# Products of zeros ahead of TensorE's first work, and behind the stages of the first two tiles

## The chip, the cores and the metric

The kernel runs on one core of one Trainium2 chip. The metric is device time in microseconds (us); lower is better. Names of engines in the profile: PE is TensorE (PEld its weight loads), DVE is VectorE, ACT is ScalarE, POOL is GpSimd, SP is the engine that issues most transfers.

## The reference, cut to what matters

Three layers follow one another: an attention-like recurrence over 768 steps (4 batches, 8 heads, head size 48), a feed-forward layer with an ELU, and a layer of 8 experts of which every token takes the best one.

```python
for t in range(S):
    kt, vt, rt, wt = (k[:, :, t], v[:, :, t], r[:, :, t], w[:, :, t])
    cur = np.einsum('bhd,bhe->bhde', u[None] * kt, vt)
    y[:, :, t] = np.einsum('bhd,bhde->bhe', rt, state + cur)
    state = wt[:, :, :, None] * state + np.einsum('bhd,bhe->bhde', kt, vt)
...
h = x @ w_in
g = np.where(h > 0.0, h, alpha * (np.exp(np.minimum(h, 0.0)) - 1.0))
return (g @ w_out).astype(np.float32)
...
h = np.maximum(x[mask] @ w1[e], 0.0)
out[mask] = gate_w[mask, None] * (h @ w2[e])
```

The weights of the feed-forward layer come as 64-bit floats and are turned into pairs of 16-bit floats on the chip.

## The kernel before

**Tiles and steps.** The recurrence is cut into 24 tiles of 128 steps by one batch (6 chunks by 4 batches). A tile goes through four steps. A1 (kind 0) forms running products of the decay by a scan (L336 on DVE, `RK`) and their inverses (L341, L342). A2 (kind 1) scales keys and queries on POOL (L386), forms the diagonal term by products of two columns (L395) and transposes the keys (L401). A3 (kind 2, the scores) multiplies keys and queries (L424) and masks the result on DVE (L433, into `Ab` or a spare place that the program calls `ohp` or `gg`). A4 (kind 3, the output) multiplies the masked scores with the values (L461), adds the state's part (L474, from the second chunk on), gathers the result on DVE (L478, `y`), turns it into the feed-forward layer's input (L485 on ACT, L487 on POOL, L363 on PE, L364 on ACT) and renews the state (L497). The products of the first eight tiles are of 32-bit floats.

**The feed-forward layer** works on groups of two tiles. A group takes eight units; a unit is 18 products of 256 columns (L514, `psf<-xT,wi`), an ELU on ACT and DVE (L520 to L524) and 12 products of 384 columns (L536, `pso<-wo,ring`). During the first group the weights are converted too, 16 pieces. A piece costs DVE two times three instructions (L275, L276, L277, from `stg` by `pso` into `sti`), and then ACT two (L289, L292) and POOL one (L293). A unit can't begin before its pieces are done.

**Order.** The code lists tile 0 and tile 1 step by step (`ORD`, with `P` for a piece of weights) and then the units of the first group, among them the steps of the tiles that follow. The framework's scheduler then sets each engine's own order by a modelled time line, and every engine runs its list strictly in that order. A row that waits holds up all that stand behind it on its engine.

**PSUM.** `psum(tag)` hands out banks by tag: two of `f`, three of `a`, one each of `o0`, `o1`, `o2`. The pieces use `o2`; the first group's outputs use `o0` and `o1`.

**Spare room.** `spare(n)` cuts columns from places that are idle in the first stage; the place that the program calls `X` (`X_101`) is one of them.

Of the kernel before, what the change touches and what calls it, by code (L numbers as in the profile page):

```python
# [49 lines left out]
def _pow2(n):  # L50
    return float(2.0 ** n)
# [77 lines left out]
def body(ctx, tc, r, k, v, w, u, w_in, w_out, mod, w_gate, bias, w1, w2, cst, out, dbg=None):  # L129
    nc = tc.nc  # L130
# [8 lines left out]
    def cc(name):  # L139
        o, n = _CW[name]  # L140
        return cs[:, o:o + n]
# [4 lines left out]
    def psum(tag):  # L146
        if tag == "o":
            tag = f"o{on_[0] % 3}"
            on_[0] += 1
        return ps.tile([128, 512], F32, tag=tag, name="ps" + tag, bufs=BK[tag])  # L150
# [34 lines left out]
    def spare(n, first=0):  # L185
        for z_, a_ in list(enumerate(arenas))[first:]:
            o = anext[z_]
            if o + n <= a_.shape[1]:
                anext[z_] += n
                return a_[:, o:o + n]  # L190
        raise ValueError(n)
# [15 lines left out]
    Ss = [p1.tile([PT, 2, QH, D], F16, name=f"Ss{i}") for i in range(1)]  # L207
    Z128 = p1.tile([PT, B, QH], F32, name="Z128")

    def setup():  # L210
        nc.scalar.preload_act_table_set("natural_log_exp_and_others")
        nc.scalar.dma_start(cs, cst)
        nc.scalar.dma_start(u2, u)
        nc.vector.tensor_copy(id16, cc("ident"))
        nc.gpsimd.memset(nel, -_pow2(PH))
        nc.vector.memset(bnd, 0.0)
        nc.vector.memset(bnd[:, 0::HW], _pow2(SR))
        nc.gpsimd.memset(run_, 0.0)

    def setup2():  # L220
        nc.vector.tensor_copy(tri16, cc("tri"))
# [84 lines left out]
    def load(i, which="wkrv"):  # L306
        c, b = divmod(i, B)
        st = T.setdefault(i, {})
        for nm, src in (("w", w), ("r", r), ("k", k), ("v", v)):
            if nm not in which or nm in st:  # L310
                continue
            if nm == "v":
                t = ev_[i] if i in ev_ else l4.tile([128, H, D], F32, tag="lv", name="lv")
            elif nm == "w":
                t = ld.tile([PT, 2, QH, HW], F32, tag="lw", name="lw")
            else:
                t = l3.tile([PT, QH, C], F32, tag="l" + nm, name="l" + nm)
            nc.sync.dma_start(t, src[i])
            st[nm] = t
# [580 lines left out]
    def moe_block(j, nt=2, hook=None, done=0, ahead=0, conv=False, load=False, x=False):  # L900
# [38 lines left out]
        if x and j == NB - 2:  # L939
            moe_gather(NB)  # L940
            moe_gather(NB + 1)
            moe_xm(NB)

    setup()
    NTL = NC_ * B
    xT = {}
# [6 lines left out]
    def at_step(kind, i):  # L953
        step(kind, i)
        if kind == (LK if i >= EAR else LE) and i + 2 < NTL:
            load(i + 2)

    def step(kind, i):
        if kind == 0:
            A1(i)  # L960
        elif kind == 1:
            A2(i)
        elif kind == 2:
            A3(i)
        else:
            g = grp[i]
            t0, nt = GR[g]
            if i == t0:
                xT[g] = b2.tile([128, 2 * KD, 128 * GT], F16, tag="xT", name="xT", bufs=4)
            A4(i, xT[g], 128 * (i - t0))  # L970

    U_ = 3.96
    start, tt = [], 0.0
# [22 lines left out]
        load(i, "w")  # L996
    for i in range(2):
        load(i)
    for u_ in range(NU + LAG):
        if u_ < NU:  # L1000
            SEQ.append((0, u_))
        if u_ >= LAG:
            SEQ.append((1, u_ - LAG))
# [4 lines left out]
    def pre(key):  # L1008
        while pq[0] <= SEQ.index(key):
            z_, i = SEQ[pq[0]]  # L1010
            (prep_out if z_ else prep_in)(i)
            pq[0] += 1
# [12 lines left out]
    for o in ORD:  # L1025
        if o == "P":
            pre((0, n_))
            n_ += 1
        else:
            at_step(int(o[0]), int(o[1:]))  # L1030
    mp = mb = None
    NG = len(GR)
    LU = (NG - 1) * NU
# [150 lines left out]
```

## Time and profile before

| what | us |
|---|---|
| three runs | 798.78, 787.71, 795.93 |
| median of the three | 795.93 |
| profiled execution, its own time | 793.34 |
| its span, first to last instruction | 791.6 |
| outside the span | 1.7 |

The profile is of one execution. Its share of busy time by engine: PE 93%, DVE 66%, ACT 62%, POOL 51%. In a timeline row the first number is the start in us from the span's start, the second the time that the merged instructions took; x is how many records there are (a product of 32-bit floats leaves two records each), and in brackets stands the engine's idle time ahead of it and what ended it. In a table of windows an engine's number is its busy time in the stretch, with the count of records, and PEclk is TensorE's granted clock as a share of full speed, where a record of it exists.

### The profile page before, as it was taken

How to read it: one execution, taken by the hardware profiler on the slowest of the kernel's cores; microseconds unless marked ns; L12 is line 12 of the kernel's file. 1: busy time of each engine (PE TensorE's matmuls, PEld its weight loads, DVE VectorE, ACT ScalarE, POOL GpSimd, SP SyncE). 2: the span in 40 equal slices, each digit the busy share in tenths (PEclk: the TensorE clock that was granted, in tenths of full speed). 3: DMA queues.
4: the chain of work that ended last, by engine and by line, in shares of the span. 5: the costliest groups of instructions: out<-in, count | busy, mean ns of one | idle time of the engine just before them, and what ended most of it. 6: DMA issues, size and time to landing. Idle time of an engine off the chain costs nothing.

```text
span 791.6 us, 17925 instructions
## 1 busy us (share of the span) xinstructions
PE 734.1 (93%) x6963; PEld 562.0 (71%) x6963; DVE 521.8 (66%) x1076; ACT 491.8 (62%) x954; POOL 403.9 (51%) x392
## 2 busy tenths in 40 slices
PE   4799999999999899999999999999995799999984
PEld 4677877877777677767776777776773577777763
DVE  6989963465766755575557544687797467766751
ACT  3577764555666566656665765567756477777852
POOL 4888884566676677747776652012016334322220
PEclk9999999999999899989999999999999799999998
DMA  9875422232213233333232111169439998998720
GB/s 282 253 229 180 141 52 59 65 81 60 70 51 76 76 76 57 77 85 66 67 72 65 22 21 32 52 194 301 165 136 348 256 279 246 288 282 234 254 108 12
DMA packets 86611, 108.29 MB, mean 137 GB/s; under 512 B 60437, under 2 KB 66618, under 8 KB 86516
## 3 DMA queue, kind: packets, MB, share of 16 engines
q1 hardware_dynamic: 82208, 96.46, 43.5%
q0 software_dynamic: 3456, 10.24, 4.4%
q8 instruction: 58, 0.95, 0.5%
q10 hardware_dynamic: 852, 0.34, 0.2%
q14 instruction: 37, 0.30, 0.1%
HBM read 83.80 MB, written 9.84 MB: 118 GB/s over the span
## 4 chain that ended last, share of the span: by engine, by line
PE 49%; DMA 11%; DVE 6%; issue 3%; ACT 2%; POOL 0%; SPq 0%; POOLq 0%; ACTq 0%
PE pso L536 13%; PE psf L514 13%; PE pso L867 8%; PE psf L847 7%; DMA out_dram<-ob,idxb 5%; PE psa L847 2%; DMA wi<-in_w_dram 2%; DMA XM<-G 1%; PE psa L427 1%; PE psa L395 1%; DMA G<-scr,idxb 1%; DVE W L839 1%; PE psa L477 1%; PE psa L497 1%; DMA SG<-in_w_dram 1%
## 5 line engine op out<-in xcount | busy, mean ns | idle before, releaser
L514 PE MATMUL psf<-xT,wi 128*128 128x256 f16 x1728 | 214.6, 279 | 1.0 <-ACT xT L364 0.9
L536 PE MATMUL pso<-wo,ring 128*128 128x384 f16 x1152 | 214.0, 331 | 0.2
L514 PEld LDWEIGHTS <-wi 128*128 128x128 f16 x1728 | 169.2, 101 | 30.5 <-issue 1.8
L536 PEld LDWEIGHTS <-ring 128*128 128x128 f16 x1152 | 112.7, 100 | 64.0 <-issue 4.6
L522 DVE SCALAR_TENSOR_TENSOR e<-e,psf 128x512 f32<-128x512 f32 x96 | 65.6, 684 | 121.0 <-ACT e L521 105.2
L847 PEld LDWEIGHTS <-W 128*128 128x128 f16 x1008 | 93.7, 99 | 32.8 <-issue 14.9
L322 POOL TENSOR_TENSOR ring<-e,ring 128x512 f16<-128x512 f32 x80 | 93.3, 1167 | 44.9 <-ACT ring L524 29.4
L867 PE MATMUL pso<-W,gg 128*128 128x384 f16 x624 | 111.0, 326 | 3.4 <-DVE gg L322 2.9
L524 ACT ACTIVATE ring<-e 128x512 f16<-128x512 f32 x96 | 60.3, 628 | 55.8 <-DVE e L522 55.1
L867 PEld LDWEIGHTS <-gg 128*128 128x128 f16 x624 | 60.2, 98 | 39.3 <-DVE gg L322 4.2
L520 ACT ACTIVATE e<-psf 128x512 f32<-128x512 f32 x96 | 56.3, 587 | 38.9 <-PE psf L514 38.6
L847 PE MATMUL psf<-XM,W 128*128 128x256 f16 (+1 forms) x540 | 62.1, 267 | 14.4 <-DMA XM<-G 12.3
L521 ACT ACTIVATE e<-e,nel 128x512 f32<-128x512 f32 x96 | 69.0, 719 | 2.3
L875 POOL DMA_INDIRECT out_dram<-ob,idxb x20 | 27.8, 1392 | 82.5 <-DVE ob L874 40.3
L839 DVE SCALAR_TENSOR_TENSOR W<-SG,W 128x768 f16<-128x768 f32 x56 | 52.9, 955 | 18.3 <-ACT W L838 17.0
L322 DVE TENSOR_TENSOR gg<-mt,gg 128x256 f16<-128x256 f32 (+1 forms) x112 | 43.8, 402 | 30.8 <-ACT gg L854 29.4
L839 DVE SCALAR_TENSOR_TENSOR W<-wi,W 128x768 f16<-128x768 f32 x56 | 52.7, 954 | 12.1 <-ACT W L838 11.0
L838 ACT ACTIVATE W<-SG 128x768 f16<-128x768 f32 x56 | 46.2, 839 | 15.1 <-DMA SG<-in_w_dram 10.9
L853 ACT ACTIVATE mt<-psf 128x256 f32<-128x256 f32 (+1 forms) x84 | 30.0, 361 | 39.2 <-PE psf L847 24.1
L838 ACT ACTIVATE W<-wi 128x768 f16<-128x768 f32 x56 | 46.0, 840 | 11.6 <-DMA wi<-in_w_dram 5.2
L371 POOL TENSOR_TENSOR rkp<-lr,lk 112x512 f32<-112x512 f32 x24 | 31.8, 1325 | 41.3 <-PE psa L395 41.3
L386 POOL TENSOR_TENSOR lk<-RK,lk 112x256 f32<-112x256 f32 x32 | 34.0, 1062 | 26.3 <-DVE RK L342 25.3
(263 smaller groups left out, 1186.1 us busy)
## 6 DMA issues: line engine op xcount, KB each, us to landing
SG<-in_w_dram SPq DMA_DIRECT2D x28, 768.0 KB
wi<-in_w_dram SPq DMA_DIRECT2D x28, 768.0 KB
stg<-in_w_in_dram SPq DMA_DIRECT2D x8, 768.0 KB
stg<-in_w_out_dram SPq DMA_DIRECT2D x8, 768.0 KB
lw<-in_w_dram SPq DMA_DIRECT2D x24, 227.5 KB
lr<-in_r_dram SPq DMA_DIRECT2D x24, 224.0 KB
lk<-in_k_dram SPq DMA_DIRECT2D x24, 224.0 KB
scr<-X SPq DMA_DIRECT2D x6, 770.0 KB
```

What stands on the lines that cost most here:

```text
L322: (nc.gpsimd if pool else nc.vector).tensor_tensor(lo, f, hi, op=ALU.subtract)
L386: nc.gpsimd.tensor_tensor(f[:, :, t_], xv, st[nm][:, :, t_], op=ALU.mult)
L514: nc.tensor.matmul(ph[:, 256 * z_:256 * z_ + 256], lhsT=wi[:, u_, a, kk, 128 * z_:128 * z_ + 128], rhs=xg[:, b_ * KD + kk, :], start=(n == ...
L520: nc.scalar.activation(e, ph, AF.Exp, scale=_pow2(-PH))
L521: nc.scalar.activation(e, e, AF.Identity, scale=_pow2(PH), bias=nel)
L522: nc.vector.scalar_tensor_tensor(e, e, 0.0, ph, op0=ALU.min, op1=ALU.max)
L524: nc.scalar.activation(hl[:, 0], e, AF.Copy)
L536: nc.tensor.matmul(po_[g][i][:, 0:DM], lhsT=hl[:, a, z_, 128 * i:128 * i + 128], rhs=wo[:, u_, b_, z_, :], start=(u_ + z_ + n == 0), stop= ...
L838: nc.scalar.activation(o_[:, 0], i_, AF.Copy, scale=_pow2(sc))
L839: nc.vector.scalar_tensor_tensor(o_[:, 1], i_, _pow2(sc), o_[:, 0], op0=ALU.mult, op1=ALU.subtract)
L847: nc.tensor.matmul(ph[:, 0:n_], lhsT=w_[:, a, kk, 128 * m:128 * m + 128], rhs=xm[:, b_ * KD + kk, 0:n_], start=(n == 0), stop=(n == 3 * KD ...
L867: nc.tensor.matmul(po[:, 0:DM], lhsT=h2[:, a, m, 128 * t:128 * t + 128], rhs=w_[:, b_, m, :], start=(m == 0 and a + b_ == 0), stop=(m == N ...
```

## The change

`spin(n)` issues n products of a tile of zeros with itself (128 rows, 128 weights, 512 columns, 16-bit floats) into bank `o1`, and nothing reads them. Eighteen stand ahead of all other work of PE, and four behind each step of kind 2 and 3 of the first two tiles: 34 in all. The zeros are written by one DVE memset.

```diff
+    zr = spare(512)
+
+    def spin(n):
+        pz = psum("o1")
+        for _ in range(n):
+            nc.tensor.matmul(pz, lhsT=zr[:, 0:128], rhs=zr, start=True, stop=True)
+
     def setup():
...
+        nc.vector.memset(zr, 0.0)
...
+    spin(18)
     for u_ in range(NU + LAG):
...
             at_step(int(o[0]), int(o[1:]))
+            if o[0] in "23":
+                spin(4)
```

The scheduler puts the rows of all engines anew; the lists differ up to about the end of the first group of the feed-forward layer, and hardly behind it. Line numbers in the changed kernel are 8 higher in the steps (L395 is L403, L424 is L432, L433 is L441, L461 is L469, L478 is L486; L275 to L277 are L283 to L285, L336 is L344).

PE, from its first work to the output of tile 0, before (`rkp` is the product of queries and keys, `u` the bonus, `gg` holds scaled keys and queries, `lv` the values):

```order
L395 MATMUL psf<-u_96,rkp 128x2 x4
L424 MATMUL psa<-gg 128x128 x8
L401 MATMUL psf<-cs,gg 128x112 x4
L395 MATMUL psf<-u_96,rkp 128x2 x4
L461 MATMUL psa<-lv,Ab 128x48 x8
```

The same place in the changed kernel, behind the eighteen (each L215 product comes with its weight load; of the four and the three one stands here):

```order
L215 MATMUL pso_133<-X_101 128x512
L403 MATMUL psf<-u_96,rkp 128x2 x4
L215 MATMUL pso_222<-X_101 128x512
L432 MATMUL psa<-gg 128x128 x8
L409 MATMUL psf<-cs,gg 128x112 x4
L215 MATMUL pso_278<-X_101 128x512
L403 MATMUL psf<-u_96,rkp 128x2 x4
L469 MATMUL psa<-lv,Ab 128x48 x8
```

Eight products of zeros now stand between PE's first work and the output of tile 0: four ahead of L432, one ahead of the second L403, three ahead of L469. Four more stand in the middle of the scores of tile 1, and four ahead of its output.

DVE, from the second mask of tile 0 to that tile's `y` and one row on, before:

```order
L433 SCALAR_TENSOR_TENSOR Ab<-psa,cs 128x512
L276 SCALAR_TENSOR_TENSOR pso_258<-stg,pso_258 128x384
L277 SCALAR_TENSOR_TENSOR sti<-stg,pso_258 128x384
L275 TENSOR_SCALAR pso_311<-stg 128x384
L276 SCALAR_TENSOR_TENSOR pso_311<-stg,pso_311 128x384
L336 SCALAR_TENSOR_TENSOR RK_97<-lw,bnd 112x520
L277 SCALAR_TENSOR_TENSOR sti<-stg,pso_311 128x384
L275 TENSOR_SCALAR pso_315<-stg 128x384
L276 SCALAR_TENSOR_TENSOR pso_315<-stg,pso_315 128x384
L336 SCALAR_TENSOR_TENSOR RK_98<-lw,bnd 112x520
L277 SCALAR_TENSOR_TENSOR sti<-stg,pso_315 128x384
L478 SCALAR_TENSOR_TENSOR y<-psa,dv 128x384
```

And in the changed kernel:

```order
L441 SCALAR_TENSOR_TENSOR Ab<-psa,cs 128x512
L283 TENSOR_SCALAR pso_288<-stg 128x384
L284 SCALAR_TENSOR_TENSOR pso_288<-stg,pso_288 128x384
L285 SCALAR_TENSOR_TENSOR sti<-stg,pso_288 128x384
L283 TENSOR_SCALAR pso_351<-stg 128x384
L284 SCALAR_TENSOR_TENSOR pso_351<-stg,pso_351 128x384
L486 SCALAR_TENSOR_TENSOR y<-psa,dv 128x384
L344 SCALAR_TENSOR_TENSOR RK_97<-lw,bnd 112x520
```

The `y` of tile 0 stands ahead of both scans now, and with two conversions (L277, now L285) done where four were.

DVE around the `y` of tile 1, before:

```order
L277 SCALAR_TENSOR_TENSOR sti<-stg,pso_446 128x384
L275 TENSOR_SCALAR pso_450<-stg 128x384
L341 SCALAR_TENSOR_TENSOR RK_98<-RK_98,psa 112x8x64
L276 SCALAR_TENSOR_TENSOR pso_450<-stg,pso_450 128x384
L342 SCALAR_TENSOR_TENSOR RK_98<-RK_98,psa 112x8x64
L336 SCALAR_TENSOR_TENSOR RK_98<-lw,bnd 112x520
L277 SCALAR_TENSOR_TENSOR sti<-stg,pso_450 128x384
L478 SCALAR_TENSOR_TENSOR y<-psa,dv 128x384
```

And in the changed kernel:

```order
L285 SCALAR_TENSOR_TENSOR sti<-stg,pso_355 128x384
L283 TENSOR_SCALAR pso_447<-stg 128x384
L284 SCALAR_TENSOR_TENSOR pso_447<-stg,pso_447 128x384
L285 SCALAR_TENSOR_TENSOR sti<-stg,pso_447 128x384
L349 SCALAR_TENSOR_TENSOR RK_98<-RK_98,psa 112x8x64
L486 SCALAR_TENSOR_TENSOR y<-psa,dv 128x384
```

Ahead of this `y` stood eight conversions of the 32 (those of L277) and five scans; now five conversions and four scans. Of the first group's last output on PE, three products of L461, eight of L474 and eight of L497 that stood behind it stand ahead of it now.

## Rows read from the trace of the kernel before

**Rows 1.** The page's first part: busy time, share, instructions.

```profile
PE 734.1 (93%) x6963; PEld 562.0 (71%) x6963; DVE 521.8 (66%) x1076; ACT 491.8 (62%) x954; POOL 403.9 (51%) x392
```

**Rows 2.** Windows: us, PE, PEld, DVE, ACT, POOL busy, PEclk, DMA share, GB/s.

```profile
60.00:80.00 20.00, 18.58 (x178) 15.31 (x176) 19.54 (x33) 15.92 (x30) 17.53 (x17) 1.00 0.50 169
100.00:120.00 20.00, 19.86 (x167) 15.25 (x168) 12.42 (x25) 11.41 (x22) 15.27 (x16) 1.00 0.19 46
```

**Rows 3.** Timeline of PE, 0 to 45 us.

```profile
10.82 1.84 PE L395 MATMUL psf<-u,rkp 112*128 112x2 f32 x8 [10.82 <-DVE RK L342]
12.59 3.09 PE L424 MATMUL psa<-gg 48*128 48x128 f32 x16
...
18.01 3.63 PE L461 MATMUL psa<-lv,Ab 128*128 128x48 f32 x16
...
33.70 1.94 PE L461 MATMUL psa<-lv,ohp 128*128 128x48 f32 x8
38.74 0.50 PE L363 MATMUL psf<-id,ohp 128*128 128x128 f16 x3 [3.10 <-ACT ohp L485]
...
41.13 4.21 PE L514 MATMUL psf<-xT,wi 128*128 128x256 f16 x19 [0.90 <-ACT xT L364]
```

**Rows 4.** Timeline of PE, 40 to 112 us.

```profile
41.13 6.99 PE L514 MATMUL psf<-xT,wi 128*128 128x256 f16 x36 [0.90 <-ACT xT L364]
48.05 1.71 PE L424 MATMUL psa<-gg 48*128 48x128 f32 x16
...
54.49 2.13 PE L514 MATMUL psf<-xT,wi 128*128 128x256 f16 x18
...
61.85 0.67 PE L497 MATMUL psa<-gg 128*64 128x48 f32 x16
...
70.28 1.88 PE L461 MATMUL psa<-lv,Ab 128*128 128x48 f32 x16
...
81.59 3.60 PE L514 MATMUL psf<-xT,wi 128*128 128x256 f16 x18
...
87.44 1.58 PE L474 MATMUL psa<-US,Tr 48*128 48x48 f32 x16
```

**Rows 5.** Windows around two falls of the granted clock; columns as in rows 2.

```profile
78.00:80.00 2.00, 1.29 (x16) 1.15 (x14) 2.00 (x3) 2.00 (x5) 2.00 (x2) 1.00 0.67 259
80.00:82.00 2.00, 2.00 (x18) 1.75 (x16) 2.00 (x5) 0.64 (x2) 1.83 (x3) 0.81 0.22 22
...
607.00:610.00 3.00, 0.10 (x1) 0.10 (x1) 2.27 (x4) 1.58 (x2) 2.31 (x3) 1.00 0.96 326
610.00:612.00 2.00, 0.00 (x0) 0.00 (x0) 0.19 (x1) 0.00 (x0) 1.70 (x2) 0.57 1.00 371
```

**Rows 6.** Timeline of DVE, 0 to 125 us, from three answers.

```profile
0.87 0.28 DVE L216 MEMSET bnd<- 112x260 uint32 x1 [0.87 <-PEq L1166]
...
16.43 0.68 DVE L433 SCALAR_TENSOR_TENSOR Ab<-psa,cs 128x512 f32<-128x512 f32 x1
...
19.75 1.24 DVE L336 TENSOR_TENSOR_SCAN RK<-lw,bnd 112x520 f32<-112x520 f32 x1 [0.40 <-ACT dg L397]
...
25.92 0.55 DVE L478 SCALAR_TENSOR_TENSOR y<-psa,dv 128x384 f32<-128x384 f32 x1
...
37.25 0.55 DVE L478 SCALAR_TENSOR_TENSOR y<-psa,dv 128x384 f32<-128x384 f32 x1
...
40.16 0.56 DVE L276 SCALAR_TENSOR_TENSOR pso<-stg,pso 128x384 int32<-128x384 int32 x1
40.75 0.55 DVE L277 SCALAR_TENSOR_TENSOR sti<-stg,pso 128x384 int32<-128x384 int32 x1
...
59.43 0.56 DVE L277 SCALAR_TENSOR_TENSOR sti<-stg,pso 128x384 int32<-128x384 int32 x1 [1.49 <-POOL wi L293]
...
106.44 0.55 DVE L277 SCALAR_TENSOR_TENSOR sti<-stg,pso 128x384 int32<-128x384 int32 x1
...
116.58 0.41 DVE L483 SCALAR_TENSOR_TENSOR y<-psa,cs,y 128x192 f32<-128x192 f32 x1
```

## The prediction

> **What bounds the kernel now.** I read the page's busy times first. PE is busy for 734.1 of 791.6 us [rows 1], so from some point on the kernel takes as long as PE's work. The windows show from where: until about 106 us DVE is as full as PE (19.54 of 20 us in 60 to 80), and from 100 on it has room (12.42 of 20) while PE has none (19.86) [rows 2]. DVE's load is the conversion of the weights, whose last row stands at 106.44 [rows 6]. So the front has two bounds at once, PE's dense work from 41.13 on and DVE's list, and what the change does is decided there.
>
> Then I read PE's timeline for the level of its clock. The window views give 1.00 for the first 45 us, but no record of the clock stands behind that: the durations speak. Sixteen records of L424 take 3.09 us at 12.59 and 1.71 at 48.05; sixteen of L461 take 3.63 at 18.01 and 1.88 at 70.28; nineteen of L514 take 4.21 at 41.13, and eighteen take 2.13 at 54.49 [rows 3, 4]. Everything up to about 47 us ran at the lower level, 1.2 GHz, and the same work later at 2.4. The rise came inside the 36 dense products that began at 41.13 and took 6.99 us [rows 4]; the stream of 32-bit products from 10.82 to 36 had not brought it.
>
> PE waits for three things in the front: nothing to do until 10.82, then 3.10 us ahead of 38.74 for the output of tile 1, and 0.90 ahead of 41.13 [rows 3]. The `y` of tile 1 at 37.25 leads to the first unit at 41.13, 3.9 us later [rows 3, 6].
>
> **The eighteen in front.** A product of 256 columns takes 4.21 / 19 = 0.22 us at the low level, so one of 512 about 0.43 (an estimate, by columns), and 0.24 at the high one. Eighteen take at most 7.7 us. They wait for a memset; the one like it stands at 0.87 for 0.28 [rows 6], so they run from about 1.4 and end by 9.2 at the latest, by 7 if the clock rises on the way. PE has no work before 10.82, and that work waits for DVE [rows 3]. Cost: nothing, hidden by that wait. Gain: only if the level that they bring is still there afterwards.
>
> **Does the level last?** Behind the eighteen PE idles for 1.6 to 4 us, then come eight records of two columns (1.84 us), then four products of zeros. No row shows this pattern. The nearest are two falls. In 78 to 80 PE was busy for 1.29 of 2 us, with transposes and the 48-row products of L424, and the clock fell inside 80 to 82 (0.81); in 607 to 610 it was busy for 0.10 of 3 us and the clock had fallen by 612 (0.57) [rows 5]. What PE does from 9 to 12 us in the changed kernel is less than what it did before the first of these falls, so I take it that the clock is back at 1.2 GHz by about 12 to 13 us. From there to the first unit the change offers bursts of four, between products that did not raise the clock before; the rise of before came only within the dense stream that began at 41.13 [rows 4]. So I take the whole front at the low level, as before.
>
> The Trainium skill bears on this. TensorE: Matmul & The Clock Gate, section Why this matters for your kernels, advises against idle gaps between bursts, since the clock then goes back to half. By that rule the gain of the eighteen is lost ahead of the first work and the sum stays that of the forecast; the trace agrees, since the clock fell behind the idle stretch at 607.
>
> **The sixteen between the stages, at the low level.** Eight of them stand ahead of the output of tile 0: 8 x 0.43 = 3.4 us. That output ended at 18.01 + 3.63 = 21.6, and now ends at about 25.0 (24 if the first records still find the high level). For PE alone this would do little. But DVE's list has changed with it: `y` of tile 0, which stood at 25.92 behind four conversions and two scans, now stands behind two conversions and no scan. A row of conversion takes 40.75 - 40.16 = 0.59 us [rows 6]. The second mask, at 16.43 before, comes about 1.1 later; with the five rows behind it DVE is at `y` at about 17.5 + 0.6 + 5 x 0.59 = 21.1, and waits there until about 25.1. That is 4.0 us of DVE, with all conversions queued behind the waiting row.
>
> The same follows for tile 1. Behind the output of tile 0 PE needs what it needed before, from 21.6 to 35.6 (33.70 + 1.94), without the waits in it about 12 us, and 8 more products of zeros, 3.4: its output ends at 39 to 40.4 instead of 35.6, and I take 39.2, near the early end, since some of it overlaps the waits. So `y` of tile 1 starts at about 39.4 instead of 37.25, later by 2.15, and the first unit at 43.3 instead of 41.13.
>
> DVE is further behind than that. At this `y` it has done five conversions instead of eight and four scans instead of five: 9 rows at 0.59 = 5.3 us and 1.24 for the scan [rows 6] are still to do. Ahead of the last conversion stand, beside these, one more L478 (0.55) and two more L483 (0.41 each): 1.4. Sum: 2.15 + 5.3 + 1.2 + 1.4 = 10.1 us later than 106.44, as long as DVE is the bound of that stretch. Three things come off. The work of PE that now stands ahead of the first group's last output is no longer behind it, where PE is the bound: 3 of 8 products of L461 (1.88 x 3/8 = 0.7), 8 of L474 (1.58) and 8 of L497 (0.67) [rows 4], 2.9 us. DVE's one long wait, 1.49 at 59.43 for POOL [rows 6], falls where DVE is late anyway: 1.5. And the high level may cover the first records and spins: up to 1. That leaves 10.1 - 2.9 - 1.5 - 0.5 = +5.2 us.
>
> Bounds: if only PE's own path counted, the first unit's delay of 2.2 would remain, and part of it is made up by a stage that waits for DVE: +1 at the low end. If neither wait nor level gives anything back, +7.5, and 2 more if the clock takes longer to rise at the first unit because the pieces of weights come late (18 products took 3.60 at 81.59 instead of 2.13 [rows 4]): +10 at the high end. The memset costs DVE about 0.3 in a wait of its own. Behind the first group the lists are the same, PE is the bound, and what is late stays late.
>
> So the profiled execution would take 793.34 + 5.2 = 798.5. The three runs lie at 787.71 to 798.78, with a median 2.6 above that execution; I set 799.
>
> **Rivals.** *The level lasts (0.20).* If the eighteen end late and the first bursts come early enough, the clock stays at 2.4 GHz, and then the sixteen cost little and do what holds it. The output of tile 0 would end at about 18.7 (L461 in 1.88, L424 in 1.71), DVE would reach each row of its new list without a wait: second mask 16.5, `y` of tile 0 at 19.9; then, to `y` of tile 1, that row (0.55), two scans (2.5), two masks (1.3), seven rows of conversion (4.1) and L341 (0.6): 28.9 instead of 37.25. The last conversion then comes 8.35 - 5.3 - 1.2 - 1.4 = 0.45 earlier, the 1.5 and the 2.9 come off as above: -4.9, or 788.5. For it: dense products did raise the clock at 41.13. Against it: the gap ahead of 10.82, which the change leaves open.
>
> The skill's page on the clock gate, same section, has the rule to warm TensorE up with products ahead of what is to run fast. The result of this rival is what that rule would give here. The trace agrees in that dense work raised the clock, and doesn't in that it fell behind stretches busier than this gap.
>
> *PE becomes the bound at the low level (0.08), slower.* The first unit starts with DVE 8.7 us behind; where each unit waits for its pieces, PE has gaps like those of 78 to 80 and the clock falls again and again. Every such stretch costs 3.60 - 2.13 = 1.5 us a unit of L514 and about as much for L536 and the tiles beside it. It decides from the point at which PE's work at the lower level is longer than DVE's list; with four such stretches on top of +5 to +7, +17 or 810.
>
> *Nothing that shows (0.10).* DVE's list finds its rows ready in another way than I count, its waits swap places, and the front ends where it did: 793 to 796. That zeros might not count as activity at all is no case of its own: the level stays low then, and the sum is that of the forecast without the 0.5.
>
> **How the numbers follow.** The forecast, level lost and +1 to +10 us, has 0.62. The runs of this kernel differ by 11 us among themselves, so no case is sharper than some 4 us. The range 789 to 808 takes in the forecast with its bounds, the case of nothing and about half of the case in which the level lasts. A difference of 2%, 16 us, is about what a measurement of this kernel can tell from no change. Faster by that needs 780, which even the lasting level doesn't give: 0.02. Slower by that needs 812, the upper part of the slow rival: 0.04. Within it: 0.94.
>
> **What the changed profile would show.** Eighteen products of 512 columns from about 1.4 us to 7 to 9, the later ones at half the spacing, and nothing until 10.8. Then L432 in about 3 us (1.7 if the level lasts). A wait of about 4 us on DVE ahead of the first L486, released by PE's L469, and of about 3 ahead of the second. The first unit at about 43, and the last conversion at about 115. I am wrong if L469 of tile 0 takes 1.9 us instead of 3.6, if DVE doesn't wait ahead of L486, or if the last conversion comes by 107.

## The result and the profile after

| | us |
|---|---|
| before, median of 20 runs | 793.36 (784.43 to 798.78) |
| changed, median of 20 runs | 800.04 (792.85 to 809.23) |
| ratio, with its 95% interval | 1.0113 (1.009 to 1.0136) |
| span of the profiled execution | 797.8 (before 791.6) |

The changed kernel is 1.1% slower, by less than the 2% that a single measurement tells from no change, but well outside the interval of this one. A ratio compares only executions within 1.5% of a kernel's fastest; for one kernel below this leaves out most of its executions, so the medians of all stand beside the ratios.

The page's first part of the changed kernel answers to [rows 1]: PE is busy for 14.2 us more, with 34 more products.

```profile
PE 748.3 (94%) x6997; PEld 569.0 (71%) x6997; DVE 524.5 (66%) x1077; ACT 490.0 (61%) x954; POOL 395.4 (50%) x392
```

PE's timeline of the changed kernel (start, duration, idle time ahead in brackets) answers to [rows 3, 4]:

```profile
1.48 5.99 PE L215 MATMUL pso<-X 128*128 128x512 f16 x18 [1.48 <-DVE X L226]
11.68 1.31 PE L403 MATMUL psf<-u,rkp 112*128 112x2 f32 x8 [4.21 <-issue]
...
14.65 3.09 PE L432 MATMUL psa<-gg 48*128 48x128 f32 x16
...
21.70 3.49 PE L469 MATMUL psa<-lv,Ab 128*128 128x48 f32 x16
...
45.10 4.00 PE L522 MATMUL psf<-xT,wi 128*128 128x256 f16 x18 [2.22 <-ACT xT L372]
...
55.28 1.05 PE L403 MATMUL psf<-u,rkp 112*128 112x2 f32 x8 [1.84 <-DVE e L530]
...
62.11 4.05 PE L522 MATMUL psf<-xT,wi 128*128 128x256 f16 x18
...
85.88 1.13 PE L432 MATMUL psa<-Tr,Tk 48*128 48x128 f32 x8 [2.15 <-ACT kf L411]
...
117.75 3.75 PE L522 MATMUL psf<-xT,wi 128*128 128x256 f16 x18
```

The eighteen run where PE had nothing to do, 0.33 us each on average. What follows takes as long as before: L432 3.09 us, L469 3.49. The first unit begins at 45.10, 4.0 later than at 41.13. Two later units still take 4.05 and 3.75 us, twice the 2.13 of [rows 4]: the clock is at its lower level there.

DVE's timeline of the changed kernel answers to [rows 6]:

```profile
25.29 0.56 DVE L486 SCALAR_TENSOR_TENSOR y<-psa,dv 128x384 f32<-128x384 f32 x1 [3.94 <-PE psa L469]
...
39.86 0.56 DVE L486 SCALAR_TENSOR_TENSOR y<-psa,dv 128x384 f32<-128x384 f32 x1 [3.08 <-PE psa L469]
...
67.64 0.69 DVE L530 SCALAR_TENSOR_TENSOR e<-e,psf 128x512 f32<-128x512 f32 x1 [3.32 <-ACT e L529]
...
122.41 0.55 DVE L285 SCALAR_TENSOR_TENSOR sti<-stg,pso 128x384 int32<-128x384 int32 x1
```

Each `y` now waits for PE, and the last conversion comes at 122.41 instead of 106.44.

The windows show what PE's clock did. First the changed kernel, then two windows of the kernel before that no row above shows (columns as in rows 2):

```profile
12.00:41.00 29.00, 28.08 (x141) 21.95 (x140) 17.15 (x28) 8.49 (x19) 14.94 (x17) 0.50 0.76 224
41.00:52.00 11.00, 7.23 (x43) 4.79 (x43) 10.31 (x16) 6.79 (x12) 7.03 (x7) 0.60 0.71 225
52.00:132.00 80.00, 74.46 (x575) 59.61 (x576) 67.23 (x120) 51.73 (x93) 63.23 (x60) 0.87 0.46 136
160.00:540.00 380.00, 373.53 (x4105) 287.37 (x4106) 238.19 (x516) 235.00 (x443) 225.90 (x233) 0.99 0.29 67
```

```profile
52.00:132.00 80.00, 78.44 (x687) 62.55 (x686) 62.58 (x113) 53.49 (x95) 62.39 (x59) 0.98 0.42 126
160.00:540.00 380.00, 370.19 (x4056) 282.38 (x4054) 239.95 (x518) 234.39 (x438) 221.41 (x227) 0.97 0.29 73
```

From 12 to 41 us the granted clock was 0.50: the level that the eighteen had brought was gone. A mean clock of 0.87 over the 80 us from 52 on means that 80 x 0.13 x 2 = 20.8 us of them lay at the lower level (3.2 before); the shares are rounded to two places, so such a figure is good to 0.8 us. Half of such time is lost while PE is busy: 8.8 us more than before. PE idled there for 5.5 us (1.6 before): 3.9 more. With the 4.0 us by which the first unit was late, the sum is 16.7. PE's own delay agrees: the 900th record of its products, those of zeros not counted, starts at 133.48 us before and at 150.16 in the changed kernel, 16.7 later, and so does the 1200th. DVE's last conversion is 16.0 late. So PE falls behind up to the end of the first group of the feed-forward layer, and about half of that is time at the lower level.

Then much of it comes back, against this execution of the kernel before. From 160 to 540 us PE got 4105 products done where 4056 were done before, at 0.99 instead of 0.97 and with 6.5 us idle instead of 9.8. The first product of the experts' layer is 7.8 us late, the end 6.2 (spans); before, then changed, in PE's timeline:

```profile
550.73 1.14 PE L847 MATMUL psf<-XM,W 128*128 128x256 f16 x9 [1.77 <-DVE e L522]
```

```profile
558.57 1.14 PE L855 MATMUL psf<-XM,W 128*128 128x256 f16 x9
```

This doesn't say that the changed kernel is fast there. Between PE's 1200th and 5300th record (166 to 558 us before) each of the thirteen other profiled executions here gains on that of the kernel before, by 5.6 to 12.5 us: it is this one execution that was slow in that stretch. Against the execution of the kernel with 160 columns (below), whose lists are those of before, the changed kernel is 15.5 us late at the last conversion, 16.6 at the first product of the experts' layer and 13.1 at the end, so there nothing comes back until the experts' layer.

### The profile page after: what moved, and what is told of

Its sections match the earlier page's. It is cut to its first block, busy times and chain, and to the rows that moved or that the text cites. A ratio compares the mean times of both kernels' runs of the same rounds, so it can differ in the third digit from the quotient of the medians.

```text
span 797.8 us, 17996 instructions
## 1 busy us (share of the span) xinstructions
PE 748.3 (94%) x6997; PEld 569.0 (71%) x6997; DVE 524.5 (66%) x1077; ACT 490.0 (61%) x954; POOL 395.4 (50%) x392
## 4 chain that ended last, share of the span: by engine, by line
PE 66%; DMA 13%; DVE 11%; issue 5%; ACT 2%; POOL 1%; SPq 0%; POOLq 0%; DVEq 0%; ACTq 0%
PE psf L522 20%; PE pso L544 19%; DMA out_dram<-ob,idxb 7%; PE pso L875 6%; PE psf L855 5%; PE psa L403 2%; PE psa L469 2%; PE psa L432 2%; PE psa L435 2%; PE psa L855 2%; DMA XM<-G 1%; PE psa L505 1%; DMA wi<-in_w_dram 1%; DVE RK L344 1%; DVE W L847 1%
## 5 line engine op out<-in xcount | busy, mean ns | idle before, releaser
L544 PE MATMUL pso<-wo,ring 128*128 128x384 f16 x1152 | 211.8, 329 | 0.1
L528 ACT ACTIVATE e<-psf 128x512 f32<-128x512 f32 x96 | 56.2, 586 | 39.3 <-PE psf L522 37.9
L883 POOL DMA_INDIRECT out_dram<-ob,idxb x20 | 26.1, 1304 | 86.3 <-DVE ob L882 39.6
L846 ACT ACTIVATE W<-SG 128x768 f16<-128x768 f32 x56 | 46.2, 839 | 17.9 <-DMA SG<-in_w_dram 12.6
```

The lines of the kernel that those rows point to most:

```text
L528: nc.scalar.activation(e, ph, AF.Exp, scale=_pow2(-PH))
L544: nc.tensor.matmul(po_[g][i][:, 0:DM], lhsT=hl[:, a, z_, 128 * i:128 * i + 128], rhs=wo[:, u_, b_, z_, :], start=(u_ + z_ + n == 0), stop= ...
L846: nc.scalar.activation(o_[:, 0], i_, AF.Copy, scale=_pow2(sc))
```

## The experiments

The theory at the start was the prediction's: the new list of DVE makes `y` wait, and the products of zeros make PE late for it. Its rivals: the list alone does it; the products alone do it. Every change of the number or the size of the products gives another list, so each kernel is known by two things: how far the conversions have come at the first two `y` (before: 4 and 8; changed: 2 and 5), and how many masks and `y` stand ahead of the last conversion (before: 19; changed: 22; an expectation below gives 18 for before, where the trace has 12 masks and 7 `y`). Low level is worked out as above for 52 to 132 us of the profiled execution.

| kernel | conversions at the two `y` | masks and `y` | low level, us | last conversion | median | ratio |
|---|---|---|---|---|---|---|
| before | 4, 8 | 19 | 3.2 | 106.44 | 793.36 | 1 |
| changed | 2, 5 | 22 | 20.8 | 122.41 | 800.04 | 1.0113 (1.009 to 1.0136) |
| eighteen alone | 2, 5 | 22 | 36.8 | 128.55 | 802.86 | 1.0103 (1.0039 to 1.0168) |
| the same again | 2, 5 | 22 | 9.6 | 115.88 | 802.35 | 0.998 (0.9926 to 1.0035) |
| fours alone | 2, 5 | 22 | 17.6 | 122.61 | 799.82 | 1.0121 (1.0071 to 1.0172) |
| 8 and twos | 2, 5 | 22 | 9.6 | 113.26 | 795.19 | 1.0064 (1.0027 to 1.0101) |
| changed, filled units | 2, 5 | 22 | 14.4 | 123.41 | 799.00 | 1.011 (1.0054 to 1.0165) |
| eighteen, filled outputs | 2, 5 | 22 | 12.8 | 114.98 | 798.32 | 1.0104 (1.0053 to 1.0156) |
| eighteen, filled units | 2, 5 | 17 | 6.4 | 104.02 | 794.84 | 1.0068 (1.0031 to 1.0105) |
| 20 alone | 3, 6 | 19 | 14.4 | 111.73 | 792.13 | 0.9981 (0.994 to 1.0023) |
| 32 alone | 3, 7 | 22 | 9.6 | 112.30 | 788.32 | 0.9969 (0.9937 to 1.0001) |
| 40 alone | 4, 8 | 17 | 14.4 | 106.66 | 791.38 | 1.0012 (0.998 to 1.0043) |
| 40 and eights | 4, 8 | 19 | 9.6 | 112.50 | 791.05 | 1.0002 (0.9968 to 1.0037) |
| 34 of 160 columns | 4, 8 | 19 | 6.4 | 106.92 | 786.88 | 0.9933 (0.9898 to 0.9967) |

Each ratio is to runs of the kernel before on the same chip, whose medians were 791.2, 791.43 and 792.52 in the three sessions.

**The eighteen alone.**

```diff
-            if o[0] in "23":
-                spin(4)
```

> The eighteen alone, without the fours. The scheduler gives DVE nearly the list of the changed kernel (y of tile 0 behind two conversions and two scans, y of tile 1 behind five and four), but no product of zeros stands between PE's first work and the outputs. Theory of the prediction (level lost before the first work; the products delay PE and the new list makes DVE wait for it): DVE waits under 1 us ahead of y of tile 0, y of tile 1 at about 36, first unit at about 40, last conversion at 110 to 114, ratio to before 1.002 to 1.006. Rival 'the new list alone does it': last conversion at about 122 and ratio 1.009 to 1.013, as in the changed kernel. Rival 'the products alone do it': first unit and last conversion within 2 us of before (41, 106), ratio 0.998 to 1.002.

The profiled execution (811.27 us) lies 17.8 us above this kernel's shortest of that session, so what is read here is a shorter one (791.34 us, from "once more" below). First PE, then DVE:

```profile
39.32 6.99 PE L522 MATMUL psf<-xT,wi 128*128 128x256 f16 x36 [0.90 <-ACT xT L372]
```

```profile
23.86 0.56 DVE L486 SCALAR_TENSOR_TENSOR y<-psa,dv 128x384 f32<-128x384 f32 x1 [3.50 <-PE psa L469]
...
115.88 0.55 DVE L285 SCALAR_TENSOR_TENSOR sti<-stg,pso 128x384 int32<-128x384 int32 x1
```

The first unit begins at 39.32, near the theory's 40, and the last conversion comes at 115.88, against 110 to 114. So being early at the first unit doesn't save the first group. The theory's first sign failed: DVE should have waited under 1 us ahead of the `y` of tile 0, and it waits for PE for 3.50 us (2.56 in the long execution), with no product of zeros in the way. PE's list is new there too: rows of L505 stand between the products of L469 that this `y` needs.

**The fours alone.**

```diff
-    spin(18)
```

> The fours alone, without the eighteen; the scheduler moves eight of the sixteen and then four more ahead of the first work and leaves four between the first work and the scores of tile 0, none behind. Theory of the prediction: about half of the delay of the changed kernel's products remains (1.7 us ahead of the output of tile 0), nothing is lost by leaving out the eighteen: ratio 1.004 to 1.009, between the eighteen alone and the changed kernel. Rival 'the new list alone does it': ratio 1.009 to 1.013. Rival 'the eighteen themselves cost': ratio 0.998 to 1.002.

1.0121: the ratio of the rival "the new list alone". The scheduler left four of the sixteen between the first work and the scores, twelve in front of all. Four products in the way did as much harm as eight, and what stands in front, eighteen or twelve, neither costs nor brings anything that shows beside it. The first `y` waits for 3.64 us here, as long as with none in the way.

**Forty, and eights behind the stages.**

```diff
-    spin(18)
+    spin(40)
...
-                spin(4)
+                spin(8)
```

> Forty in front, so that they end at about 12.3 us, at PE's first work, and eight instead of four behind each of the four stages. DVE's list in front stands near that of the kernel before (y of tile 0 behind four conversions and scans, y of tile 1 behind eight and five). Rival of the prediction 'the level lasts': a record of the clock at 1.00 goes on past 20 us, the products of L432 take 1.7 us instead of 3.09, L469 of tile 0 1.9 instead of 3.5, the first unit begins by 39, ratio 0.992 to 0.998. Theory 'bursts between such products don't hold the level': the clock is back at 1.2 GHz by about 16 us, the eights then take 3.4 us each, L469 of tile 0 takes 3.5, and the ratio is 1.005 to 1.015.

PE's timeline of this kernel, and then DVE's:

```profile
13.00 1.71 PE L432 MATMUL psa<-gg 48*128 48x128 f32 x16
...
19.60 1.92 PE L469 MATMUL psa<-lv,Ab 128*128 128x48 f32 x8
...
33.66 0.99 PE L469 MATMUL psa<-lv,ohp 128*128 128x48 f32 x8
...
43.28 3.69 PE L522 MATMUL psf<-xT,wi 128*128 128x256 f16 x18 [1.81 <-ACT xT L372]
```

```profile
26.88 0.55 DVE L486 SCALAR_TENSOR_TENSOR y<-psa,dv 128x384 f32<-128x384 f32 x1
...
37.84 0.57 DVE L486 SCALAR_TENSOR_TENSOR y<-psa,dv 128x384 f32<-128x384 f32 x1
```

With dense products right up to the first work the higher level is there for it (L432 in 1.71 us), is lost by 19.60 (eight records in 1.92), is back at 33.66 (eight in 0.99) and lost again by 43.28. Neither expectation of the time came: 32 products between the stages, part of them at the lower level, cost nothing, and the level in the front brought nothing. Neither `y` waits for PE here, because DVE has four and eight conversions to do ahead of them. So the products' own time counts at most where the list makes DVE wait for it.

**Forty alone.**

```diff
-    spin(18)
+    spin(40)
...
-            if o[0] in "23":
-                spin(4)
```

> Forty in front and none behind the stages: the dense products reach the first work, DVE's list stands near that of before. Theory: the level lasts for the first products alone (L432 in 1.7 us) and is gone by about 16 us; since DVE has its own list to do, y of tile 0 and the first unit come when they came before (25 to 26, 40 to 42), ratio 0.997 to 1.003. Rival 'a gap ahead of the first work is all that undid the level': the level holds to 20 us or longer, the first unit comes before 39, ratio under 0.996.

```profile
13.84 1.71 PE L432 MATMUL psa<-gg 48*128 48x128 f32 x16
```

The ratio and the level came as the theory had it. But the first `y` stands at 27.62 and the first unit at 45.92, later than it said and later than in the changed kernel, and still the last conversion comes at 106.66: the first unit's time isn't what decides either. The windows show the level there for the first work and gone by the next stretch:

```profile
12.00:20.00 8.00, 4.90 (x40) 4.20 (x38) 5.51 (x11) 1.33 (x3) 4.46 (x7) 0.84 1.01 331
20.00:41.00 21.00, 15.71 (x94) 13.84 (x92) 17.54 (x29) 11.36 (x23) 15.38 (x15) 0.50 0.85 246
```

**Which part of the list? Twenty alone, thirty-two alone** (the edit of the forty with another number).

> Twenty in front and no fours. The scheduler's list for DVE is new in the front (y of tile 0 behind three conversions and three scans, y of tile 1 behind six and four), but in the first group's stretch it is near that of before: 19 masks and y stand ahead of the last conversion (18 before, 22 in the changed kernel and with the eighteen alone), the third tile's second pair of masks behind 19 and 20 conversions (20 before, 16 and 17 there). Theory A, the front's order costs (y ahead of conversions): last conversion at 118 or later, ratio 1.006 to 1.012. Theory B, the order in the first group's stretch costs (rows of later tiles ahead of conversions, PE's gaps and the falls of its clock): last conversion at 106 to 112, ratio 0.998 to 1.004. In both the products themselves cost nothing.

> Thirty-two in front and no fours: the other half of the pair. DVE's list in the front is near that of before (y of tile 0 behind three conversions and three scans, y of tile 1 behind seven and five), but in the first group's stretch it is as new as in the changed kernel: 22 masks and y ahead of the last conversion. Theory A (front): last conversion at 106 to 112, ratio 0.998 to 1.004. Theory B (first group's stretch): last conversion at 118 or later, 15 us or more of the lower clock level between 41 and 130 us (3.4 before), ratio 1.006 to 1.012.

Neither theory alone: the twenty came as theory B said (last conversion at 111.73, 0.9981), the thirty-two within 0.3 us and 0.0011 of what theory A said (112.30, 0.9969), and each result is far from the other theory's. Neither kernel loses, so neither a partly new front nor a new first group is enough by itself. Their `y` stand in between, at 3 and 6, and 3 and 7, so the front is not quite as new as in the changed kernel, nor quite as before. What can be said is that 22 masks and `y` ahead of the last conversion are not enough for a loss, and three and six conversions at the two `y` aren't either.

**Dense products in the first group.** The changed kernel and the eighteen alone, with four dense products that nothing reads ahead of each unit of the first group:

```diff
         xg = xT[g]
+        for _ in range(4 if g == 0 else 0):
+            nc.tensor.matmul(ph[:, 0:256], lhsT=id16, rhs=xg[:, 0, :], start=True, stop=True)
```

> The changed kernel with four dense unread products of 256 columns ahead of each of the eight units of the first group, 32 in all, 3.5 us of PE at the high level. DVE's list stays that of the changed kernel up to the third tile and has 22 masks and y ahead of the last conversion as there. Theory 'the falls of the clock in the first group are what costs most' (20.4 us at the low level there, half of it lost): if the fill keeps the level, 10 us or less of low level remain between 41 and 130, the first group's last output comes at 124 to 130 instead of 131.6, ratio to before 1.002 to 1.009. Rival 'the falls only show where PE waits anyway': the fill adds its 3.5 us, ratio 1.013 to 1.018.

> The eighteen alone, and four dense unread products ahead of each unit of the first group. The front of DVE's list is word for word that of the eighteen alone (y of tile 0 behind two conversions and two scans, y of tile 1 behind five and four), but the fill has moved the rows of later tiles back: 17 masks and y ahead of the last conversion instead of 22. Theory A (front): last conversion at 118 or later, ratio 1.008 to 1.014. Theory B (first group's stretch): last conversion at 104 to 112, ratio 0.998 to 1.005.

In the changed kernel the fill took the low level from 20.8 to 14.4 us, worth 3.2, and its own 32 products cost 3.8 (2.13 / 18 = 0.118 us each, [rows 4]): 1.011, no change, between the two expectations. In the eighteen alone it moved rows as well: the last conversion came at 104.02, as theory B said, and the ratio of 1.0068 is 1.002 once the fill's 3.8 us are taken off. That is nearer to theory B, but the fill keeps it from being clean.

**All 34, of 160 columns.** The lists of DVE (one memset apart), ACT, POOL and SP are then those of before from end to end, and so is PE's behind the 34, which all stand in front.

```diff
-            nc.tensor.matmul(pz, lhsT=zr[:, 0:128], rhs=zr, start=True, stop=True)
+            nc.tensor.matmul(pz[:, 0:160], lhsT=zr[:, 0:128], rhs=zr[:, 0:160], start=True, stop=True)
```

> All 34 products, but of 160 columns instead of 512: the scheduler then leaves the lists of DVE, ACT and POOL word for word as before and puts all 34 ahead of PE's first work, where PE idles. Theory 'the products cost nothing, the list does': last conversion at 106 to 108, 3.4 to 7 us of low level between 48 and 130 us, ratio 0.997 to 1.003. Rival 'products of zeros cost in themselves': ratio 1.004 or more. It also shows a second execution of the list of before: if the later falls of the clock (176.8, 262.1, 347.5, 432.8 before) are the list's own they stand at the same places, if not, elsewhere.

The products cost nothing: last conversion at 106.92. Yet the ratio is 0.9933, faster than expected and faster than both kernels. Its windows:

```profile
52.00:132.00 80.00, 78.48 (x674) 62.94 (x675) 62.33 (x115) 54.32 (x97) 63.28 (x60) 0.96 0.44 131
160.00:540.00 380.00, 372.84 (x4128) 286.61 (x4127) 244.39 (x527) 240.65 (x448) 225.74 (x231) 0.99 0.32 78
```

```profile
541.97 1.14 PE L855 MATMUL psf<-XM,W 128*128 128x256 f16 x9
```

The gain stands in 160 to 540 us: 4128 products against 4056, at 0.99 against 0.97, with identical lists. Of the four later falls of before, this execution has none near 347.5 and 432.8; it has one at 167.2 and one at 262.8. So those falls are not all the list's own, and the time that the changed kernel got back in that stretch needs no new list and no late front as its cause. Why this kernel loses less of the higher level there is open.

**The eighteen alone, once more** (no edit).

> The eighteen alone once more, for a profile of another execution. Theory 'a list that is new in the front and in the first group makes PE wait and its clock fall there': 15 us or more of low level between 48 and 130 us again (37.5 in the first profile), first group's last output at 125 to 135, ratio 1.007 to 1.014. Rival 'the 30.7 us of low level from 90 us on belong to that one execution': 10 us or less, first group's last output before 122.

The rival came, for the profile: an execution of 791.34 us, with 9.6 us of low level and the first group's last output at about 122.6, a little past the 122 asked for. The medians of all executions are the same in both sessions, 802.86 and 802.35, since 11 of the 18 took more than 800 us (before, the highest of 29 in that session is 801.57). The two executions of this one program, first the long one, then the short one, in two windows each:

```profile
92.00:122.00 30.00, 30.00 (x163) 23.73 (x163) 21.54 (x43) 12.80 (x23) 16.72 (x19) 0.52 0.51 144
52.00:132.00 80.00, 75.68 (x520) 60.44 (x520) 63.99 (x109) 47.36 (x85) 54.18 (x53) 0.77 0.42 127
```

```profile
92.00:122.00 30.00, 28.05 (x222) 22.38 (x222) 24.42 (x46) 19.75 (x33) 21.87 (x22) 0.93 0.39 111
52.00:132.00 80.00, 73.61 (x614) 58.33 (x614) 68.04 (x116) 52.72 (x93) 60.38 (x58) 0.94 0.42 127
```

And what stands ahead of it in PE's timeline, in the long and in the short one:

```profile
90.81 1.94 PE L482 MATMUL psa<-US,Tr 48*128 48x48 f32 x8 [3.45 <-DVE y L486]
```

```profile
87.48 1.09 PE L482 MATMUL psa<-US,Tr 48*128 48x48 f32 x8 [3.45 <-DVE y L486]
```

The same wait of 3.45 us for DVE's `y`, then 30 us at 0.52 in the one and at 0.93 in the other. The list sets the wait; how long the lower level lasts behind it differs from one execution to the next.

**The eighteen, with dense products at that wait.**

```diff
             pi = [psum("a") for _ in range(2)]
+            for _ in range(24 if i < 8 else 0):
+                nc.tensor.matmul(pi[0][:, 0:128], lhsT=id16, rhs=id16, start=True, stop=True)
```

> The eighteen alone, with 24 dense unread products of 128 columns ahead of the state's part of the output (the line of psa<-US,Tr) of tiles 4 to 7, where PE has just waited for y and the clock has fallen: 1.3 us of PE at the high level each, 5.3 in all. DVE's list is that of the eighteen alone for its first 121 rows (to about 90 us) and near it behind. Theory 'the low level there is what costs': the fall that begins near 90 lasts 10 us or less instead of 30.7, the first group's last output comes at 120 to 128 instead of 134.7, ratio 1.002 to 1.009. Rival 'the wait for DVE costs, the level only shows it': the products add their 5 us, ratio 1.013 to 1.018.

In PE's timeline the products stand where the wait was, and it is gone:

```profile
84.34 1.50 PE L480 MATMUL psa<-id 128*128 128x128 f16 x24
85.77 0.64 PE L484 MATMUL psa<-US,Tr 48*128 48x48 f32 x4
```

The last conversion came at 114.98, and the median of all executions is 798.32, 4 us below that of the eighteen alone although 5.3 us of products were added. The fall near 90 lasts 3.4 us. The ratio of 1.0104 lies between the two expectations. It speaks for the theory, but the list behind row 121 has changed as well, so it doesn't settle it.

**Eight, and twos behind the stages.**

```diff
-    spin(18)
+    spin(8)
...
-                spin(4)
+                spin(2)
```

> Eight in front and two behind each of the four stages, 16 in all instead of 34. The scheduler's list for DVE is new in both parts: y of tile 0 behind two conversions and two scans, y of tile 1 behind five and four, 22 masks and y ahead of the last conversion. Theory 'a list new in both parts costs, whatever the products': last conversion at 118 or later, 15 us or more of low level between 48 and 130 us, ratio 1.007 to 1.014. Rival 'the cost goes with the number of products': ratio 1.001 to 1.006.

1.0064, between the two. The low level of 9.6 us and the last conversion at 113.26 are those of the short execution of the eighteen alone, not what the theory asked for.

**The lower level in all executions.** The low level in the table above is of one execution each, and there it doesn't sort the kernels: 9.6 us with the eight and twos, which lose, and with the thirty-two, which don't. But every execution has its span and its mean granted clock on record, so its time at the lower level can be estimated: 2 x (1 - clock) x span, less the stretch in front that its kernel's profile shows (34.1 to 41.0 us, 13.7 with the forty and eights), for which the kernel before has no record of the clock. The medians of all executions, each less that of the kernel before in the same session (for the changed kernel less 37.9 us, from the other sessions' 0.976):

| kernel | more low level, us | half of it | longer by, us |
|---|---|---|---|
| changed | 12.5 | 6.2 | 6.7 |
| eighteen alone | 24.9 | 12.4 | 11.7 |
| the same again | 24.0 | 12.0 | 9.8 |
| fours alone | 17.9 | 9.0 | 8.6 |
| 8 and twos | 6.3 | 3.1 | 2.7 |
| 20 alone | 6.2 | 3.1 | 0.7 |
| 32 alone | -2.1 | -1.0 | -3.1 |
| 40 alone | 0.7 | 0.4 | 0.2 |
| 40 and eights | 2.1 | 1.0 | -0.2 |

Half of the added low level is the added time within 2.4 us in each. In the three kernels with dense products of their own it has nearly gone (-2.8 to 3.2 us), and their products' time with half of that is the added time within 3.6 us. The 160 columns are left out: the mean clocks of their executions fall into two kinds (0.944 to 0.960, 0.970 to 0.985) at about the same times.

Together: all kernels that have the changed kernel's front (2 and 5) and its 22 masks and `y` lose 0.6 to 1.2% by their ratios, the eighteen alone by one of their two; by the medians of all executions 0.3 to 1.5%. No kernel without both loses more than 0.12%, the one with a fill of its own apart. This holds whether none, 4 or 16 products stand between the stages, and 32 between them cost nothing with the front of the list of before. The eighteen, twenty, thirty-two and forty alone differ only in how many products fill PE's idle time in front, and in the lists that come with them. So the cause is the order that the scheduler makes of the change, and its price, by this estimate, is time at the lower clock level. Which rows do it is not shown: the two marks are of DVE's list, and PE's list is new as well. Nor is it shown for every kernel that the added low level lies in the first group. That a list without any product of zeros, but with this order, would lose the same was not tried.

## Why the prediction was right, and where it wasn't

The forecast of 799 stands against 800.04. That it came so near is luck in part: two errors of opposite sign.

- **The eighteen, hidden.** Forecast from about 1.4 to between 7 and 9.2 us at no cost; they ran from 1.48 to 7.47.
- **The level is lost.** Forecast back at 1.2 GHz by 12 to 13 us; the window from 12 to 41 has 0.50. The forty with eights speaks against the -4.9 us of the rival in which it lasts: it had the level for a good part of the front and stands at 1.0002, since DVE had conversions of its own to do ahead of each `y`.
- **The rule of the skill.** The forty alone had the level at their first work (L432 in 1.71 us, and 3.09 behind the gap in the changed kernel). By that the Trainium skill (TensorE: Matmul & The Clock Gate, section Why this matters for your kernels) is right that an idle gap between bursts takes the level back and that products ahead of the work bring it. The advice to warm up, which the Trainium skill gives there for measuring, gains nothing here (1.0012), because PE doesn't bound this stretch.
- **The waits.** Forecast 4.0 us at the first `y`, at 25.1, and about 3 at the second, at 39.4; they are 3.94 at 25.29 and 3.08 at 39.86. But my sum laid the first on the products' 3.4 us, and they are neither enough nor needed for it: with the list of before, twice the products made no `y` wait, and with the new lists of the eighteen alone the `y` of tile 0 waits 3.50 us with none in the way.
- **The first unit.** Forecast 43.3, came at 45.10: 1.8 too small. 0.5 comes from the second `y`, the rest from the way from there to the unit: 5.2 us instead of the 3.9 taken from before, with 2.22 of wait for ACT's `xT` at its end. The runs also showed that this step doesn't carry the outcome: first unit at 39.32 and last conversion at 115.88 with the eighteen alone, 45.92 and 106.66 with the forty.
- **The last conversion: the term that was mis-sized.** Forecast at about 115 (10.1 late, less 1.5 for DVE's wait), and it came at 122.41, 16.0 late. The deduction of 1.5 us for DVE's wait was wrong: another wait of 3.32 us (for `e` at 67.64) took its place. And the sum left out the clock in the first group, which I had put into the slow rival at 0.08: 20.8 us at the lower level there, against 3.2. That rival's mechanism took part in the outcome, if not at its price of 17.
- **What is late stays late: open.** Against the profiled execution of the kernel before it fails: PE is 16.7 us late behind the first group and 7.8 by the first product of the experts' layer. I had taken off 2.9 for PE's work done early (not measured apart). But that execution got fewer products done in 160 to 540 us than any other here, and against the execution with 160 columns, at lists like those of before, the delay stays until the experts' layer. What I had wrong was to take the stretch behind the first group of one execution as fixed.

So +5.2 was forecast and +6.2 found between the profiled executions, but through +16 in front and -10 behind, not through +10.1 and -4.9; and the -10 belongs in large part to the execution that I measured against. The loss over all executions, 6.7 us by the medians, is matched by half of the 12.5 us of lower level that the changed kernel has more, a term that my sum left out.

## What to carry to other kernels

Where a scheduler orders the engines by modelled times, an added instruction acts through the order first: compare the lists, and find a version of the change that leaves them as they were (here 160 columns instead of 512) before its own time is argued about. Ask of a late stage which gaps it opens on the engine with the throttled clock, since the lower level behind a gap can cost more than the gap. And PE's time in a stretch can be split into idle time, half of the time at the lower level, and work: the first two explain a difference between two kernels of the same work, without a chain. The mean clock gives the second for every execution, and one profiled execution as the only measure of a kernel misleads: here the one of the kernel before was slow in a stretch that the change doesn't touch.

## What the runs showed of the hardware that was not expected

- One program, two executions, 20 us apart (811.27 and 791.34): behind the same wait of 3.45 us PE's clock stayed at the lower level through almost all of 92 to 122 us in one (0.52), and through little of it in the other (0.93).
- In that long stretch PE was busy for 30.00 of 30 us and the level still didn't rise, with 163 products where the other execution did 222; from 12 to 41 us of the changed kernel it was busy for 28.08 of 29 at 0.50. Busy time in the profile doesn't say that the level will rise.
- Products of zeros do bring the level: L432, the same sixteen records, took 1.71 us with forty of them up to the first work, and 3.09 where PE had idled for 4.21 us behind eighteen.
- What sets the executions of one program apart here is the lower level: the changed kernel took 792.85 us at a mean clock of 0.953 and 809.23 at 0.934, about 32 us more of the lower level and 16.4 us more time.
- Two kernels with the same lists from end to end, one with 34 small products in idle time, differ by 0.67% (0.9898 to 0.9967). An effect under 1% on this kernel can't be put down to an edit by its time alone.
